# Weight sums for two units at once, sums as single steps, a narrower U-product, and a new order, in a kernel of local attention and a two-layer mixer

## The chip, the cores and the metric

The kernel runs on one core of one Trainium2 chip. The time is device microseconds of one execution. The kernel before took 217.62 us (median of 3 runs, 217.62 to 218.74). Its profiled execution took 217.54 us, of which 215.8 us lie between the first and the last recorded instruction (the span). The granted clock of TensorE was 1.000 in it.

## The reference

Attention over 4 batches of 8 heads, 768 positions and head size 64; each query sees the first 8 positions and the 96 up to its own, with a bias per head. Then a mixer over the 768 positions: a low-rank product with U (768 x 32) and V (32 x 768), and a two-layer MLP with 2048 hidden units.

```python
scores = scale * q @ k.T + bias                  # per head; bias = -slope * distance
scores = where(is_global | is_local, scores, -1e9)
a = softmax(scores)
x = (a @ v)                                      # heads side by side: (4, 768, 512)
h = x.transpose(0, 2, 1) @ U @ V
u = x + h.transpose(0, 2, 1)
out = u + relu(u @ w_ch1) @ w_ch2                # w_ch1: 512 x 2048, w_ch2: 2048 x 512
```

Inputs and output are float32; the kernel computes in fp16 with float32 accumulation.

## The kernel before

**How the order comes about.** The program makes a list of named tasks, each on one engine. `ORDER` is a written list of all names, and the instructions are issued exactly in this order: each engine takes its own in that sequence, and waits where data or a buffer is missing. `SLOTS` gives each task that takes a buffer or a PSUM bank the number of it. `CFG` names by one letter the engine (A for ACT, D for DVE, S for SyncE's DMA queue) of each movable task. A change of order is therefore a change of these three lists. The durations in the calls of `add` steer nothing on the chip.

**Attention**, for 16 pairs p of heads (four per batch). `lk`, `lq` and `lv` load k, q and v (POOL issues; pair 0's k and q come over SyncE). `Ck0` and `Cq0` cast pair 0. `TK` and `TQ` transpose on TensorE into PSUM and `EK`, `EQ` copy out (pairs 8 to 15 are transposed by DMA instead); `KO`, `VC` and `VG` build shifted copies with the global keys. `SB` adds the bias (batch 0), `S` makes scores in PSUM (line 652), `EX` is the exponential (ACT, line 717), `MK` the mask on DVE, `PV` the product with v (lines 780 and 781), `RC` and `NM` the normalization (DVE, lines 815 and 819), `XC` the cast to fp16.

**The low-rank mixer**, per pair. `UP` multiplies with U: six matmuls (line 764) with the 128-column U tile `uz` as the stationary and the 128 columns of x as the moving operand, which leave U^T x with 128 rows in PSUM; in batches 0 and 1 six more (line 759) transpose x. `TE` copies the result into `tmp` (ACT or DVE), `HM` multiplies with V (line 871), and `E0`, `E1` add or copy the sum into `uT`. In batches 2 and 3 `XT` transposes x by DMA.

**MLP-1** makes 16 blocks of 128 hidden units for 768 positions, in halves of 384. Plain blocks are `M1a` to `M1d` with relu `RL`, `RM` (batch 0 but for one unit). The others go in units z, each for the blocks z and z + 8, by a scheme of seven products instead of eight (`ZP1` to `ZP7`, two matmuls of 384 columns each, line 1024). It needs sums of the inputs (`ZT`, four DVE instructions in one task per batch, lines 979 to 982) and sums of the weights (`ZS`, four DVE instructions per unit, lines 1000 to 1003; made once per unit and kept). `ZU`, `ZW`, `ZX` and `ZR` copy PSUM out on ACT; `ZA`, `ZB` and `ZD` add with relu on DVE (line 1042) and free the bank.

**MLP-2** uses the same scheme once more: `PA` and `PB` (two DVE instructions each, four groups per batch) make sums of the relus, `TWa`, `TWb` sums of the second weights, `RS` starts the banks, `P1` to `P7` are products of eight matmuls each (line 1141), `DA` to `DH` add into the output on DVE (lines 1153, 1193), and `O` stores. `w` tasks are filler matmuls on zeros (line 1240).

```python
def sums_s(...):                     # ZS, one unit
    op(sw(2), a11, a21, ALU.subtract)
    op(sw(0), a21, a22, ALU.add)
    op(sw(1), sw(0), a11, ALU.subtract)
    op(sw(3), a12, sw(1), ALU.subtract)
```

Of the kernel before, what the change touches and what calls it, by code (L numbers as in the profile page):

```python
# [21 lines left out]
lk0 ones2 ones3 vz wz iota w6 lq0 ones0 relf w1 lk1 w4 rel3 bias1 bias0 w2 lq1 w0 w3 lk3 mask3 SB0.2 Ck0.0 Ck0.1 vs1  # L22
mask1 TK0 lv0 w7 Cq0.0 EK0.1 SB0.0 w5 mask7 lk2 Cq0.1 bias2 EK0.0 TQ0 lq3 SB0.1 KO0.1 EQ0.1 ones1 EQ0.0 KO0.0 lq2
S0.2 TK1 EX0.2 lv1 S0.1 EK1 TQ1 EX0.1 S0.0 lv2 EQ1 TK3 EX0.0 SB1.0 KO1 u16 SB1.1 bias4 S1.1 VC0 EK3 S1.0 vs0 uz SB1.2
VG0 lv3 EX1.0 KO3 S1.2 TK2 EX1.2 PV0 EK2 EX1.1 lk5 TQ3 RC0 NM0 TQ2 EQ3 SB2.1 KO2 SB2.2 EQ2 SB2.0 VC1 lk4 S2.0 VG1
S2.1 XC0 EX2.0 S2.2 PV1 EX2.2 VC2 lq4 SB3.1 uc EX2.1 RC1 back S3.1 mixl NM1 SB3.2 EX3.1 S3.2 VG2 lq5 SB3.0 VC3 VG3
S3.0 mask0 TK5 EX3.0 PV2 EK5 w1_1 EX3.2 PV3.0 RC2 UP0 RC3.0 w1_7 NM2 XC1 TK4 PV3.1 w1_5 TE0 EK4 PV3.2 XC2 HM0 RC3.1
lv4 RC3.2 UP1 NH3.1 E00 NH3.0 UP2 NM3 w1_3 TE1 UP3.0 TE2 UP3.1 NH3.2 w1_2 KO4 HM1 HM2 E01 TQ5 E02 w1_4 UP3.2 TQ4 TE3
EQ5 lk6 M1a0.3 EQ4 M1c0.3 HM3 S4.1 E13 E03 M1d0.3 EX4.2 lv5 ZT0 M1a0.2 M1c0.2 M1b0.3 EX4.1 w1_0 M1a0.15 RL0.3 M1b0.14
VC4 KO5 M1a0.14 RM0.14 w1_6 vs2 RL0.15 M1d0.2 mask2 S5.0 S4.0 M1b0.2 EX4.0 M1a0.11 EX5.0 MK4.0 M1b0.7 lk7 VG4 RL0.2  # L30
M1a0.7 MK4.2 RM0.7 MK4.1 M1b0.15 RL0.14 ZS3 M1b0.10 RL0.11 mask5 M1b0.6 MK5.0 RL0.7 RM0.15 lq7 ZS7 S5.1 RM0.10
M1b0.11 EX5.2 ZS6 PV4 w2_3 EX5.1 M1a0.10 lq6 RM0.11 M1b0.8 MK5.1 RM0.6 M1a0.8 RC4 RL0.10 NM4 VC5 ZP10.5 w2_1 ZP20.5
RM0.8 ZS5 M1a0.6 ZU0.5 RL0.8 M1a0.1 MK5.2 w2_2 mask6 TK6 M1c0.1 RL0.6 EK6 w2_0 ZP60.5 M1d0.1 TD0 ZW0.5 PA0.3 M1b0.1
lv6 VG5 M1b0.12 PA0.1 ZP50.5 RM0.12 M1b0.4 RL0.1 TK7 ZA0.5 RM0.4 ZP70.5 lq8 PB0.1 PV5 mask4 KO6 M1a0.5 EK7 ZX0.5 RC5
M1a0.4 lk9 NM5 RL0.5 TQ6 RL0.4 TQ7 ZB0.5 KO7 M1a0.12 EQ6 XC5 M1a0.0 EQ7 M1c0.0 lv8 PB0.3 ZP40.5 XC4 ZP30.5 M1d0.0
RL0.12 ZD0.5 M1b0.0 ZR0.5 M1b0.5 RL0.0 PA0.2 S7.0 lv7 RM0.5 UP4 EX7.0 PA0.0 S6.1 TE4 RS0.1 EX6.2 HM4 PB0.2 P20.1 E04
PB0.0 UP5 EX6.1 P10.1 TWa1 lk8 TE5 S6.0 RS0.0 EX6.0 HM5 DA0.1 P20.0 TWa0 lv9 VC6 P30.0 E05 lq10 TWb0 P50.0 VG6 P50.1
TWb1 lq9 P30.1 DF0.0 P60.1 MK6.1 TK8 P10.0 DF0.1 lk10 ZS2 S7.1 VG9 EX7.1 RS0.2 MK6.0 P10.2 DA0.0 EX7.2 MK6.2 P20.2
TQ8 DC0.1 VC7 PV6 MK7.2 VG7 TK9 P60.0 DB0.1 MK7.0 DA0.2 P70.1 RC6 TQ9 DB0.0 MK7.1 P60.2 DD0.1 NM6 PV7 TQ10 P40.1 RC7
XC6 NM7 VC9 lq12 P30.2 DB0.2 XC7 VG8 ZS4 UP6 KO8 UP7 lv11 DG0.1 DF0.2 TE6 P70.0 TE7 ZS1 lk11 HM7 HM6 S8.0 E07 E06  # L40
P50.2 DD0.0 lv14 DC0.0 E17 ZP11.6 KO9 ZT1 ZP11.7 lk12 P70.2 ZU1.7 ZU1.6 ZP21.7 EX8.0 P40.0 lq11 ZA1.7 ZP61.7 DG0.0
# [30 lines left out]
ZP53.4 ZR3.5 ZP53.7 ZX3.4 ZP23.3 ZB3.7 ZP13.0 ZR3.2 ZP63.3 ZB3.4 ZP63.1 ZA3.3 ZP23.2 ZP33.7 ZU3.0 ZA3.2 ZP53.2 ZW3.1
ZP43.4 ZD3.7 ZP33.4 TD3 ZW3.3 ZP23.1 ZD3.4 ZP63.0 ZP73.1 ZA3.1 ZW3.0 ZP53.1 ZB3.2 ZX3.1 ZP73.3 ZP73.0 PA3.3 ZX3.3
ZP23.0 ZR3.4 ZP33.2 ZP53.0 ZX3.0 ZB3.1 ZP53.3 ZD3.2 ZP43.3 ZP33.1 ZB3.0 ZR3.3 ZP43.0 ZB3.3 ZP43.1 ZR3.0 ZP33.0 ZD3.1
ZR3.1 ZP33.3 ZA3.0 RS3.0 RS3.2 ZD3.3 RS3.1 ZD3.0 P23.2 PA3.2 P13.0 PA3.0 P23.1 PA3.1 P23.0 P13.1 PB3.1 P53.2 DA3.1
DA3.0 P13.2 PB3.3 P63.0 DF3.2 PB3.0 P53.0 DA3.2 PB3.2 P63.1 O3.2a O2.2 P63.2 DB3.0 O2.5 O2.3 P53.1 DB3.2 O2.0 P33.1
DB3.1 P73.2 DF3.1 P33.2 DC3.2 DD3.2 P33.0 DC3.0 O3.5a P73.1 DF3.0 P73.0 O3.0 DD3.1 DC3.1 P43.2b DH3.2 O3.1 P43.1
DG3.2b DD3.0 O3.2 P43.2a O3.5c DG3.1 P43.0 O3.4 DG3.2a O3.5b w18 w8 DG3.0 w13 w11 O3.3 w17 w21 w14 w9 w15 w12 w16 w22
w19
""".split()  # L80
CFG = {
# [82 lines left out]
def kernel(  # L164
# [1127 lines left out]
```

## Time and profile before

| | |
|---|---|
| median of 3 runs | 217.62 us |
| profiled execution | 217.54 us |
| its span | 215.8 us |
| TensorE busy | 211.1 us (98%) |
| weight loads | 153.7 us (71%) |
| DVE busy | 189.3 us (88%) |
| ACT busy | 138.2 us (64%) |
| POOL busy | 72.2 us (33%) |

In the rows, a line begins with the line of the kernel, then the engine and the operation, what is written and read, the shape, the count, and then busy time and the mean of one in ns. In a timeline the first number is the start in us from the span's start and the second the duration. The chain of waits lists pieces as start, duration, and what ran. Matmuls are pipelined and their ends are modelled: a matmul's mean duration is longer than the distance from its start to the next one's.

### The profile page before, as it was taken

How to read it: one execution, taken by the hardware profiler on the slowest of the kernel's cores; microseconds unless marked ns; L12 is line 12 of the kernel's file. 1: busy time of each engine (PE TensorE's matmuls, PEld its weight loads, DVE VectorE, ACT ScalarE, POOL GpSimd, SP SyncE). 2: the span in 40 equal slices, each digit the busy share in tenths (PEclk: the TensorE clock that was granted, in tenths of full speed). 3: DMA queues.
4: the chain of work that ended last, by engine and by line, in shares of the span. 5: the costliest groups of instructions: out<-in, count | busy, mean ns of one | idle time of the engine just before them, and what ended most of it. 6: DMA issues, size and time to landing. Idle time of an engine off the chain costs nothing.

```text
span 215.8 us, 5747 instructions
## 1 busy us (share of the span) xinstructions
PE 211.1 (98%) x2298; PEld 153.7 (71%) x2298; DVE 189.3 (88%) x417; ACT 138.2 (64%) x255; POOL 72.2 (33%) x95
## 2 busy tenths in 40 slices
PE   8998999999999989999999999999999999999996
PEld 3565855676889866566787875667789766668896
DVE  4687977999999998999999899999999975999680
ACT  6999989989924669789886467785722068730000
POOL 8989967873670860013961100000000000000000
DMA  6999999999999999779999957651002310000543
GB/s 166 175 168 156 145 180 177 181 194 196 154 151 157 147 156 159 179 185 127 141 132 129 121 155 144 185 94 36 3 0 51 74 49 3 2 2 3 219 149 122
DMA packets 100731, 26.78 MB, mean 124 GB/s; under 512 B 87744, under 2 KB 98112, under 8 KB 100704
## 3 DMA queue, kind: packets, MB, share of 16 engines
q0 software_dynamic: 71312, 13.34, 80.1%
q1 hardware_dynamic: 29392, 13.07, 28.3%
q8 instruction: 18, 0.29, 0.6%
q14 instruction: 9, 0.07, 0.1%
HBM read 27.56 MB, written 6.29 MB: 157 GB/s over the span
## 4 chain that ended last, share of the span: by engine, by line
PE 91%; ACT 5%; DVE 2%; issue 1%; POOL 0%; POOLq 0%
PE ps L1141 35%; PE ps L1024 26%; PE ps L927 6%; PE ps L652 4%; ACT ep L717 4%; PE ps L1240 3%; PE ps L951 3%; PE ps L764 3%; PE ps L781 2%; PE ps L780 2%; PE ps L521 2%; PE ps L871 2%; PE ps L759 1%; PE ps L1133 1%; PE ps L633 1%
## 5 line engine op out<-in xcount | busy, mean ns | idle before, releaser
L717 ACT ACTIVATE ep<-ps 128x1024 f16<-128x1024 f32 (+1 forms) x48 | 43.9, 957 | 13.3 <-PE ps L652 12.5
L1141 PEld LDWEIGHTS <-htr 128*128 128x128 f16 x392 | 36.3, 98 | 7.3 <-issue 2.3
L265 ACT ACTIVATE zu<-ps 128x384 f32<-128x384 f32 x59 | 27.5, 491 | 8.5 <-PE ps L1024 7.6
L1042 DVE CUSTOM_DVE_ANT_0 htr<-ps,zu 128x384 f16<-128x384 f32 x59 | 31.0, 551 | 1.0 <-PE ps L1024 0.4
L1153 DVE TENSOR_TENSOR x_sb<-x_sb,ps 128x256 f32<-128x256 f32 (+1 forms) x60 | 27.1, 463 | 3.6 <-PE ps L1141 3.1
L1141 PEld LDWEIGHTS <-sA 128*128 128x128 f16 x288 | 27.5, 98 | 3.6
L364 POOL DMA_DIRECT2D vt<-in_v_dram x16 | 16.5, 1032 | 31.7 <-PE ps L781 22.4
L1024 PEld LDWEIGHTS <-w 128*128 128x128 f16 x200 | 18.9, 98 | 11.3 <-issue 0.2
L1141 PE MATMUL ps<-tB,htr 128*128 128x256 f16 (+1 forms) x200 | 24.0, 268 | 0.0
L1141 PE MATMUL ps<-w,sA 128*128 128x256 f16 x192 | 23.6, 273 | 0.0
L1141 PE MATMUL ps<-w,htr 128*128 128x256 f16 x192 | 23.5, 273 | 0.0
L360 POOL DMA_DIRECT2D stgq<-in_q_dram x24 | 19.9, 854 | 10.1 <-DMA qT<-stgq 7.2
L1024 PE MATMUL ps<-uT,w 128*128 128x384 f16 x100 | 23.0, 326 | 0.0
L1024 PE MATMUL ps<-zt,w 128*128 128x384 f16 x100 | 22.6, 326 | 0.0
L360 POOL DMA_DIRECT2D stgk<-in_k_dram x24 | 20.4, 872 | 4.1 <-DMA w<-in_moe_w_ch_dram 2.5
L265 ACT ACTIVATE x<-x_sb 128x768 f16<-128x768 f32 x13 | 10.9, 845 | 10.4 <-DVE x_sb L819 10.3
L730 DVE TENSOR_TENSOR ep<-ep,mask 128x1024 f16<-128x1024 f16 x24 | 16.3, 684 | 0.5 <-ACT ep L717 0.5
L819 DVE TENSOR_TENSOR x_sb<-ps,rcp 128x768 f32<-128x768 f32 x16 | 15.2, 952 | 0.3
L1024 PE MATMUL ps<-zt,zs 128*128 128x384 f16 x64 | 15.3, 326 | 0.0
L927 PE MATMUL ps<-uT,w 128*128 128x384 f16 x80 | 14.7, 326 | 0.0
L652 PE MATMUL ps<-qT,kT 64*128 64x128 f16 x192 | 14.1, 217 | 0.0
L652 PE MATMUL ps<-qT,kO 64*128 64x128 f16 x160 | 12.8, 218 | 1.0 <-DVE htr L1042 0.7
(119 smaller groups left out, 408.6 us busy)
## 6 DMA issues: line engine op xcount, KB each, us to landing
out_dram<-x_sb SPq DMA_DIRECT2D x20, 256.0 KB, 2.4
vt<-in_v_dram POOLq DMA_DIRECT2D x16, 192.0 KB, 7.0
stgk<-in_k_dram POOLq DMA_DIRECT2D x24, 96.0 KB, 6.0
stgq<-in_q_dram POOLq DMA_DIRECT2D x24, 96.0 KB, 5.6
w<-in_moe_w_ch_dram POOLq DMA_DIRECT2D x8, 256.0 KB, 8.6
w<-in_moe_w_ch_dram POOLq DMA_DIRECT2D x4, 512.0 KB, 9.8
out_dram<-x_sb SPq DMA_DIRECT2D x7, 128.0 KB, 2.2
vo<-vt SPq DMA_DIRECT2D x5, 123.8 KB, 2.5
```

Of the source, the lines that this page charges most:

```text
L265: nc.scalar.activation(dst, src, AF.Copy)
L360: nc.gpsimd.dma_start(o[:, i], src[b, h0 + i].rearrange("(n p) d -> p n d", p=P))
L364: nc.gpsimd.dma_start(vt[gv.slot][:, :, :, 0:D], v[b, h0:h0 + 2].rearrange("h (n p) d -> p h n d", p=P),)
L652: nc.tensor.matmul(t[:, hi, j * P:(j + 1) * P], lhs, qt[r, i * P:(i + 1) * P], start=not biased, stop=True, skip_group_check=biased,)
L717: nc.scalar.activation(ep[gep.slot][:, :, lo:512], ps[:, gsc.slot:gsc.slot + 2, lo:512], AF.Exp, scale=qk_scale)
L730: nc.vector.tensor_tensor(ev, ev, mv, ALU.mult)
L819: nc.vector.tensor_tensor(xo, pvo()[:, :, :, 0:D], rcp[p % 2].unsqueeze(3).broadcast_to((P, 2, NB, D)), ALU.mult)
L927: nc.tensor.matmul(ps[:, g.slot, 0:HS], w1[:, dc, jt * P:(jt + 1) * P], ub[:, dc, i * HS:(i + 1) * HS], start=(dc == 0), stop=(dc == NDC - 1),
L1024: nc.tensor.matmul(bank(g), a()[:, i], bq[:, i], start=first and i == 0, stop=last and i == 1, skip_group_check=True,)
L1042: return lambda: nc.vector._custom_dve(TENSOR_ADD_SAT, out=o, in0=x(), in1=y(), s0=3.0e38, s1=0.0)
L1141: nc.tensor.matmul(o if part is None else o[:, part], a[:, j, c0 + cols.start:c0 + cols.stop], bq[:, j] if part is None else bq[:, j, part ...
L1153: nc.vector.tensor_tensor(o, o, x, ALU.add)
```

## The change

- **Weight sums for two units.** The four steps of `ZS` become four tasks `ZYa` to `ZYd`, each for two neighbouring units (512 columns rather than 256), so 16 instructions instead of 32. They are kept in four tiles; `zt` takes over the early scratch space that lay in `once`.
- **Single steps.** `ZT` becomes `ZTa` to `ZTd`, `PA` and `PB` become `PA` to `PD`, `TWa` and `TWb` become `TWa` to `TWd`: the same instructions, each a task of its own in the order, and each product waits for the step it needs rather than for all.
- **The U-product with 32 moving columns**, for pairs 4 to 15 (`XU` in `CFG`): x is the stationary operand and 32 columns of U the moving one. `XE` (ACT, for pair 6 DVE) copies the 128 x 32 result four times side by side into `tmp`, `XU` turns it by one matmul with the identity, and `TE` copies as before.
- **A new order**, new slots and engines. Masks 0 and 1 stand ahead of the first exponential (before: 3, 1 and 7), the others in batch 0's MLP-1; `bias4` stands ahead of the first exponential.

```diff
+                    if xu:
+                        nc.tensor.matmul(
+                            ps[:, gx.slot, 384:384 + R], xx[:, c], uz[:, c, 0:R],
+                            start=xt and c == 0, stop=(c == NB - 1), skip_group_check=True,
+                        )
+                for c in () if xu else cs:
                     nc.tensor.matmul(
                         ps[:, gx.slot, 384:512], uz[:, c], xx[:, c],
...
+        if xu:
+            def xuevac():
+                copy(ENG[CFG["XE"][p]], tm.rearrange("p (g r) -> p g r", r=R), ps[:, gx.slot, 384:384 + R].unsqueeze(1).broadcast_to((P, P // R, R)))
+            def xuturn():
+                nc.tensor.matmul(ps[:, gx.slot + 1, 384:512], tm, ident16, start=xt, stop=True, skip_group_check=True)
+            XE = add(ENG[CFG["XE"][p]], 0.28, xuevac, [UP] + xw, name=f"XE{p}")
+            UP = add(PE, 0.06, xuturn, [XE], lat=0.3, name=f"XU{p}")
...
-            ZT = add(DVE, 2.21, sums_t, dd(range(NDC)) + zt_read, fast=32, name=f"ZT{b}")
+            for n, x, ch, dp in ((0, "a", (0, 1), ()), (2, "c", (0, 1, 2, 3), ()), (1, "b", (2, 3), (0,)), (3, "d", (2, 3), (1,))):
+                ZT[n] = add(DVE, 0.55, sums_t(n), dd(ch) + [ZT[i] for i in dp] + zt_read[n], fast=2, name=f"ZT{x}{b}")
...
+                for x, o, i0, i1, op in (
+                    ("a", zy[:, 1], c11, c21, ALU.subtract), ("b", c21, c21, c22, ALU.add),
+                    ("c", zy[:, 0], c21, c11, ALU.subtract), ("d", zy[:, 2], c12, zy[:, 0], ALU.subtract),
+                ):
...
+            for x, o, i0, i1, op, dp in (
+                ("A", s1, a21, a22, ALU.add, r21 + r22 + war(5)), ("C", s2, s1, a11, ALU.subtract, r11 + war(6)),
+                ("B", a21, a11, a21, ALU.subtract, r11 + r21), ("D", s4, a12, s2, ALU.subtract, r12 + war(3)),
+            ):
...
-    "TE": "AAADAAAAAAADAAAD", "EK": "ADDADDDDAADDAADD", "EQ": "DDAADADDADAAAAAA", "KO": "ADDDADAAAAAASSAD", "IB": "AAAA",
+    "TE": "DAADDAAAAADAAAAA", "EK": "ADDDADAAAADDAADD", "EQ": "DAAADDDAADAAAAAA", "KO": "AADDDDDAADAAAAAS", "IB": "AAAA",
-    "KOS": "DDDADADA", "VO": "DDDDDAAASSASASAS", "XC": "DAADAAAAAAAAAAAD", "E": "ADADAAADDDDDDDDD",
+    "KOS": "DDDADADA", "VO": "DDDDDAAAASASDDSA", "XC": "DDADDAAAAADAAAAA", "E": "AAADAAADDDDDDDDD",
```

The places of the order that the prediction's steps speak of, before and after (single lines of `ORDER`, cut):

```diff
-... TK0 lv0 w7 Cq0.0 EK0.1 SB0.0 w5 mask7 lk2 Cq0.1 bias2 EK0.0 TQ0 lq3 ...
+... w1 mask1 TK0 Cq0.0 Cq0.1 EK0.0 TQ0 EK0.1 lk2 KO0.0 SB0.0 ...
-... lv3 lk5 ... lk4 ... lq4 ... lq5 ... w1_1 w1_7 w1_5 lv4 ...          (POOL's loads)
+... lv3 lk4 lk5 w1_1 lq4 w1_7 lq5 w1_3 lv4 ...
-... HM7 HM6 S8.0 E07 E06 P50.2 DD0.0 lv14 DC0.0 E17 ZP11.6 KO9 ZT1 ZP11.7 ...
+... HM6 HM7 E06 ZYb0 ZP11.7 E07 P70.2 E17 DF0.2 ZU1.7 ZP21.7 O0.2 S8.0 ZA1.7 ZP11.6 EX8.0 VG9 lk15 ZTb1 ...
+... UP4 PD0.1 RM0.5 TWb0 lq8 S7.0 XE4 EX7.0 XU4 S6.1 TE4 PA0.2 HM4 ...
-... P43.2b DH3.2 O3.1 P43.1 DG3.2b DD3.0 O3.2 P43.2a O3.5c DG3.1 P43.0 O3.4 DG3.2a O3.5b w18 w8 DG3.0 w13 w11 O3.3 ...
+... O3.2 DG3.2a O2.4 P43.2b DD3.0 P43.1 O3.5b DG3.2b O3.5c P43.0 O2.1 DG3.1 O3.4 w19 w16 DG3.0 w9 w17 O3.3 ...
```

More of the change, by code (lines that the diff above doesn't have):

```diff
@@ L21 @@
 ORDER = """
[L22 to L41, printed above, removed]
@@ L72 @@
[L72 to L76, printed above, removed]
@@ L77 @@
-DB3.1 P73.2 DF3.1 P33.2 DC3.2 DD3.2 P33.0 DC3.0 O3.5a P73.1 DF3.0 P73.0 O3.0 DD3.1 DC3.1 P43.2b DH3.2 O3.1 P43.1
-DG3.2b DD3.0 O3.2 P43.2a O3.5c DG3.1 P43.0 O3.4 DG3.2a O3.5b w18 w8 DG3.0 w13 w11 O3.3 w17 w21 w14 w9 w15 w12 w16 w22
-w19
+lk0 wz iota w2 lq0 relf w4 lq1 w0 rel3 bias0 bias1 w7 lk1 bias2 w3 ones0 w5 lk3 mask0 SB0.2 Ck0.1 bias4 ones1 lv0
+Ck0.0 w1 mask1 TK0 Cq0.0 Cq0.1 EK0.0 TQ0 EK0.1 lk2 KO0.0 SB0.0 EQ0.1 KO0.1 SB0.1 lq3 EQ0.0 vz S0.2 lq2 EX0.2 TQ1 S0.0
+lv1 EQ1 TK1 SB1.2 EX0.0 EK1 vs1 S0.1 ones2 TK3 ones3 uz lv2 KO1 w6 EK3 SB1.0 EX0.1 S1.2 u16 S1.0 VC0 SB1.1 EX1.0 vs0
@@ new lines @@
+TK2 VG0 lv3 EX1.2 S1.1 EK2 PV0 EX1.1 TQ3 RC0 KO2 TQ2 NM0 lk4 SB2.2 EQ2 SB2.1 VC1 EQ3 SB2.0 VG1 S2.0 S2.1 lk5 EX2.0
+S2.2 KO3 PV1 XC0 EX2.1 RC1 SB3.1 uc EX2.2 w1_1 SB3.0 VC2 NM1 S3.0 S3.1 lq4 EX3.0 SB3.2 VG2 S3.2 EX3.1 VC3 UP0 XC1
+w1_7 EX3.2 PV2 TE0 VG3 lq5 TK4 RC2 PV3.0 NM2 EK4 PV3.1 PV3.2 TK5 RC3.0 RC3.1 XC2 HM0 RC3.2 w1_3 EK5 UP1 NH3.2 back
+E00 mixl lv4 UP2 NH3.0 NH3.1 TE1 UP3.0 NM3 TE2 w1_5 HM1 HM2 E01 UP3.1 KO4 lk7 UP3.2 TQ4 E02 TE3 M1a0.3 EQ4 M1c0.3
+ZTa0 HM3 S4.1 E13 E03 M1d0.3 EX4.2 KO5 M1a0.2 ZTc0 M1b0.3 lk6 M1c0.2 mask5 TQ5 RL0.3 M1a0.15 EQ5 mask6 M1a0.14 w1_6
@@ new lines @@
+EX4.1 M1b0.14 VC4 w1_2 RL0.15 M1d0.2 RM0.14 M1b0.2 w1_4 RL0.14 S4.0 ZYa3 S5.0 M1b0.6 ZYa1 EX5.0 M1a0.7 EX4.0 M1b0.15
+mask2 lq6 MK4.0 RL0.7 M1b0.11 vs2 RM0.15 M1b0.7 RL0.2 VG4 lv5 M1b0.10 MK4.1 RM0.6 mask3 S5.1 RM0.11 w1_0 MK5.0
+M1a0.10 RM0.7 ZYb3 RM0.10 lq7 PA0.1 TK6 EX5.1 M1a0.11 PC0.1 TK7 EX5.2 MK5.1 M1a0.4 w2_0 MK4.2 EK7 M1a0.5 w2_2 ZYa2
+PV4 RL0.11 MK5.2 w2_1 RL0.4 M1a0.6 PA0.3 RL0.10 w2_3 RC4 EK6 M1b0.12 PB0.3 NM4 VC5 lv10 M1a0.8 TQ6 TD0 VG5 ZTb0
+M1a0.12 RL0.6 PB0.1 PV5 RL0.5 XC4 mask4 EQ6 ZP10.5 RL0.12 M1b0.8 lk8 KO6 RM0.12 ZYb2 RL0.8 M1a0.1 ZYc3 M1c0.1 ZU0.5
@@ L872, in hmix @@
                     ps[:, gx.slot + half, 0:HS], tmp[b % 2][r, hp * P:(hp + 1) * P], vs[r, half],
-                    start=xt and half == 1, stop=True, skip_group_check=True,
+                    start=xt and not xu and half == 1, stop=True, skip_group_check=True,
                 )
@@ L1019, in bank, with pr @@
                 return ps[:, g.slot, 0:HS]
-            def pr(n, g, a, bq, dp, reads=False, first=False, last=False, z=z, gs=gs):
+            def pr(n, g, a, bq, dp, reads=False, first=False, last=False, z=z):
                 def go():
```

273 lines of the change are left out of this document (138 added, 135 removed), and 12 rows, old and new, of the table CFG.

## The prediction

> **What bounds the kernel now.** I read the page's first and fourth part, then the windows by stage, then the chain of waits, and where the chain leaves TensorE the timelines.
>
> ```profile
> span 215.8 us, 5747 instructions
> PE 211.1 (98%) x2298; PEld 153.7 (71%) x2298; DVE 189.3 (88%) x417; ACT 138.2 (64%) x255; POOL 72.2 (33%) x95
> ...
> PE 91%; ACT 5%; DVE 2%; issue 1%; POOL 0%; POOLq 0%
> ```
>
> TensorE carries the kernel; but DVE at 88% is close behind, and the chain leaves TensorE for ACT (5%, about 11 us) and for DVE (2%, about 4 us). The windows (busy us of PE, PEld, DVE, ACT, POOL) say where:
>
> ```profile
> 8.00:20.00 12.00, 11.72 (x217) 7.19 (x214) 10.28 (x25) 11.41 (x15) 10.57 (x14) 1.00 2.12 170
> 20.00:27.00 7.00, 6.56 (x123) 5.81 (x124) 5.76 (x15) 6.53 (x13) 7.00 (x10) 1.00 1.62 143
> 27.00:54.00 27.00, 27.00 (x280) 17.41 (x278) 23.80 (x58) 25.50 (x51) 17.73 (x22) 1.00 1.69 186
> 54.00:76.00 22.00, 21.96 (x272) 18.61 (x269) 21.48 (x49) 12.78 (x21) 12.90 (x16) 1.00 1.98 152
> 76.00:102.00 26.00, 25.18 (x230) 15.83 (x228) 24.52 (x54) 21.21 (x46) 5.83 (x7) 1.00 1.24 162
> 102.00:128.00 26.00, 25.96 (x334) 20.91 (x331) 24.75 (x48) 17.80 (x28) 11.31 (x14) 1.00 1.79 129
> ...
> 192.00:211.00 19.00, 19.00 (x187) 17.00 (x184) 15.94 (x36) 0.00 (x0) 0.00 (x0) 1.00 0.31 113
> ```
>
> From 8 to 20 us ACT is the fuller engine (11.41 of 12), and TensorE's 11.72 is many short matmuls whose modelled ends overlap. From 27 us on TensorE has no gap, except between 76 and 102 us (25.18 of 26). From 54 to 128 us DVE is 94 to 98% busy. So three things can shorten this kernel: fewer TensorE instructions after 20 us, less ACT work before 20 us, and less delay on DVE in the middle.
>
> **The change, part by part.** The sum is made against the profiled execution, 217.54 us, of which 215.8 are span; the median of the runs is 217.62, so the two stand for each other.
>
> *a. TensorE's work.* The rows are pieces of the chain (start, us, what, number of matmuls):
>
> ```profile
> 21.57 0.09 PE ps L781 x3
> ...
> 22.15 0.34 PE ps L764 x6
> ...
> 63.61 0.55 PE ps L652 x16
> ...
> 73.52 0.87 PE ps L1141 x8
> ...
> 210.76 3.06 PE ps L1240 x52
> ```
>
> The U-product of a pair is six matmuls of 128 moving columns, 0.34 us (L764), 0.057 each. With 32 columns the trace shows none; the nearest is PV with 65 columns, 0.03 each (L781), each with a weight load of its own. A matmul of 32 columns costs between 0.014 (a quarter of 0.057) and 0.057 (were the load the floor); I take 0.03, since the 65-column row shows that loads do not hold it above that. Twelve pairs: 12 x (0.34 - 0.18) = 1.9 us less. The turn back (XU) adds one matmul of 128 columns to each: 12 x 0.057 = 0.7. One filler task more (w15) stands in mid-order instead of behind the last product: four matmuls at 3.06/52 = 0.06, so 0.2. Sum -1.0; bounds +0.9 and -2.0. The Trainium skill, "TensorE: Matmul & The Clock Gate", on why the gap is 56 ns, puts a floor of about 25 ns under start-to-start however few the columns. By it the six would take an estimated 0.15 and this term be -1.4; no row here goes below 65 columns. The same page of the Trainium skill, on the back-to-back gap, gives about 81 ns per matmul for a stream of weight loads and matmuls of 128 columns. Row L764, with a load for each, shows 57, and the trace decides.
>
> *b. The first 20 us, ACT.* Pieces of the chain:
>
> ```profile
> 6.34 0.41 PE ps L1240
> ...
> 10.75 0.52 ACT once L316
> 11.26 0.70 ACT kT L265
> ...
> 15.91 0.48 issue
> ...
> 19.95 0.41 ACT mask L1228
> ```
>
> The new order puts TQ0 straight behind its casts, not behind a 512-column filler (-0.41). bias4 (-0.52) goes ahead of the first exponential, where ACT waits anyway; mask0 takes mask3's early place and leaves 19.95 (-0.41); EK3 goes to DVE (-0.70). EQ2 stands before EQ3, so that S2.0 no longer waits for the later of them (-0.48). Against that EQ1 and KO1 come to ACT:
>
> ```profile
> L265 ACT ACTIVATE qT<-ps 128x768 f16<-128x768 f16 x3 | 2.4, 847 | 0.0
> L265 ACT ACTIVATE kO<-kT 128x480 f16<-128x480 f16 x8 | 4.8, 602 | 0.0
> L265 ACT ACTIVATE kO<-kT 128x160 f16<-128x160 f16 x8 | 2.7, 333 | 0.0
> ```
>
> As back-to-back work I take 0.70 for EQ1 (the chain's piece for EK3, same shape) and 0.85 for KO1, a little under 0.60 + 0.33: +1.55. The sum is -0.97. Loads must follow: w1_1, which the first MLP-1 tile needs, moves ahead of lq4 and lq5 in POOL's queue, so it comes earlier, and they later; TQ4 and TQ5 stand later too. I take -0.9; bounds 0 (a load or the casts hold the stage) and -2.5 (EQ1 and KO1 fit into waits).
>
> *c. DVE, single steps and wider sums.* The timelines, DVE first, then TensorE (start, us):
>
> ```profile
> 78.30 0.55 DVE L981 TENSOR_TENSOR zt<-uT 128x768 f16<-128x768 f16 x1
> 78.77 0.55 DVE L982 TENSOR_TENSOR zt<-uT,zt 128x768 f16<-128x768 f16 x1
> 79.23 0.55 DVE L1042 CUSTOM_DVE_ANT_0 htr<-ps,zu 128x384 f16<-128x384 f32 x1
> ...
> 81.15 0.29 DVE L1001 TENSOR_TENSOR w<-w 128x256 f16<-128x256 f16 x1
> 81.47 0.29 DVE L1002 TENSOR_TENSOR once<-w 128x256 f16<-128x256 f16 x1
> 81.80 0.29 DVE L1003 TENSOR_TENSOR once<-w,once 128x256 f16<-128x256 f16 x1
> 82.01 0.55 DVE L1042 CUSTOM_DVE_ANT_0 htr<-ps,zu 128x384 f16<-128x384 f32 x1
> ```
> ```profile
> 78.95 0.23 PE L652 MATMUL ps<-qT,kO 64*128 64x128 f16 x1
> 79.83 0.21 PE L652 MATMUL ps<-qT,kO 64*128 64x128 f16 x1 [0.65 <-DVE htr L1042]
> ...
> 83.53 0.23 PE L652 MATMUL ps<-qT,kO 64*128 64x128 f16 x2 [0.17 <-DVE x_sb L1153]
> ```
>
> A step that needs the one just before it starts 0.32 to 0.33 after it (81.15, 81.47, 81.80); an unrelated one follows after 0.21 (82.01). So each dependent neighbour costs 0.11. A ZS of one unit holds DVE for 3 x 0.32 + 0.21 = 1.2 us, eight of them 9.4. Two units at once make 16 steps of 512 columns, an estimated 0.34 each (between 0.21 for 256 and 0.47 for 768, 78.30 to 78.77): 5.4, thus 4.0 less. In the new order only three steps stand right behind one that they need, of PA to PD, ZT and TW; the old PA and ZT had twenty such places, 2.2 us. The changed engine choices (four pieces of EK, EQ and E off DVE, some nine short ones of VO, XC, KO, TE and XE onto it) I count as nil. About 6 us of 189 go, all off the chain but in one place: at 78.95 S8.0 waits 0.65 for a bank that ZA1.7 (L1042) frees, which stood behind the ZT1 steps; at 83.53 S8.1 waits 0.17. In the new order S8.0 stands ahead of ZA1.7, and ZP5 waits for one step of ZT alone. I take -0.8 for these two and -0.5 for the hidden remainder of 54 to 128 us, where DVE had 1 to 6% of slack; bounds 0 and -2.5.
>
> *d. The second trip.* UP now goes through XE, XU and TE to HM. Before XU can start, UP's last matmul must end and XE run:
>
> ```profile
> L764 PE MATMUL ps<-x,uz 128*128 128x128 f16 x96 | 8.2, 219 | 0.0
> L265 ACT ACTIVATE tmp<-ps 128x128 f16<-128x128 f32 x13 | 3.7, 282 | 4.3 <-PE ps L764 4.2
> L717 ACT ACTIVATE ep<-ps 128x1024 f16<-128x1024 f32 x32 | 31.6, 1027 | 11.2 <-PE ps L652 10.9
> ```
>
> That is 0.22 + 0.28 = 0.50 us. TensorE's cover between UP and XU is one MLP-2 product (0.87) for pairs 5, 7, 9, 10, 11, 13 and 15, several ZP for 8 and 12, some 0.6 for 14; for pair 4 only S7.0, six matmuls at 0.034 (0.2): 0.3 uncovered. XE6 stands on DVE behind TWd0 and two more; 0.1 for it. Sum +0.4; bounds 0 and the rival below. XE also adds 11 x 0.28 = 3.1 us to ACT, idle for a third of the span.
>
> *e. The end.* Behind the last RS, DVE has 13 single steps of PA to PD among the DA and DB that free the banks; P63.2 waits for DA3.2, which stands behind five others after the last PC. DVE had 15.94 of 19.00 there, so the cover is thin: +0.3, bounds 0 and +1.0. The stores O2.0, O2.4 and O2.1 (256 KB each) move in among the last of SP's queue:
>
> ```profile
> out_dram<-x_sb SPq DMA_DIRECT2D x20, 256.0 KB, 2.4
> ```
>
> O3.4 and O3.3 wait behind O2.1. Its issue falls in the time of P43.0 (0.87), so I take nothing; if data queues, at most its 2.4.
>
> Sum: -1.0 - 0.9 - 1.3 + 0.4 + 0.3 = -2.5, **215.0 us** (span 213.3).
>
> **Rivals.**
>
> *Everything comes through.* The middle loses all 2.5 of c, ACT's stage 1.5, and the trip costs nothing: -1.0 - 1.5 - 2.5 + 0.3 = -4.7, 212.8. For it: 54 to 128 us has two full engines now. Against: few gaps are left to close. Chance 0.12.
>
> *ACT takes over in batch 0's MLP-1, and the gain stays there.* From 27 to 54 us ACT has 25.50 of 27.00. Between EX4.2 and RM0.5 the new order adds two masks, EK6, EK7 and EQ7, and takes out KO6, XC4 and XC5:
>
> ```profile
> L1228 ACT ACTIVATE mask<-once 128x384 f16<-128x384 f16 x8 | 4.3, 537 | 0.8 <-DVE once L304 0.8
> L265 ACT ACTIVATE kT<-ps 128x768 f16<-128x768 f16 x1 | 0.8, 823 | 0.0
> L265 ACT ACTIVATE x<-x_sb 128x768 f16<-128x768 f32 x13 | 10.9, 845 | 10.4 <-DVE x_sb L819 10.3
> ```
>
> That is 2 x 0.54 + 2 x 0.82 + 0.85 - 0.94 - 2 x 0.85 = +0.9, so 26.4 of 27. It decides where a relu comes late by more than its bank's turn. Then b's 0.9 is waited out there, and up to 1.0 on top: 217.54 - 2.5 + 1.9 = 216.9. The same place holds the case that the change doesn't do what it says: 32 columns cost 0.057 each, term a is +0.9, and the time 216.9. The PV row speaks against that. Chance of both, 0.16.
>
> *Slower: XE waits behind exponentials.* ACT takes its instructions in order; an exponential (1.03) just ahead of XE makes the trip 1.53, of which 0.87 is covered: 0.66 per pair. Without d the sum is -2.9; the loss must pass 4.0, so it decides at six of twelve pairs. At eight it is 5.3: 217.54 - 2.9 + 5.3 = 219.9. For it: ACT waited 4.2 us for just such products (L265 tmp), so the chain is short of slack. The Trainium skill, "Perfetto Trace Analysis", on the Tensor Engine instruction in its lifecycle part, says that ACT's and DVE's queues never reorder; the wait at 78.95, behind DVE's steps, agrees. The order speaks against it: an exponential stands directly ahead of XE only at pairs 5 and 11. Chance 0.14.
>
> **How the numbers follow.** A measurement here can tell about 0.5%, 1.1 us, from no change. Forecast 0.58 (213.4 to 216.5), everything 0.12, ACT or no saving 0.16, slower 0.14. So faster 0.58 + 0.12 = 0.70, the same 0.16, slower 0.14. The range leaves out the slower case and half of the first rival: 212.8 to 217.9.
>
> **What would show it.** Right: L764's successor takes 0.18 us for six; MLP-1's first piece starts about 0.9 us earlier; no wait of S8 on L1042; DVE's busy time 1 to 3 us lower, with fewer starts 0.32 apart; XU shows gaps of 0.3 at pair 4 only. Wrong: TensorE waiting for XE at several pairs, ACT full with TensorE gaps from 27 to 54 us, TensorE gaps after 190 us, or 32-column matmuls at 0.05.

## The result, and the profile after

The changed kernel takes 215.65 us (median of 18 runs, 215.01 to 217.62), the kernel before 217.82 (18 runs beside it, 217.39 to 221.14): ratio 0.9899, 95% interval 0.9879 to 0.9918. It is about 2.2 us faster; 215.0 was forecast.

The first profiled execution of the changed kernel was the slowest of its 18 (217.62 us), so the lines here are those of another execution of the same kernel, which took 215.56 us, unless the text says otherwise. Line numbers are those of the changed kernel: scores 654, UP's transposition 762 and its 32-column matmul 767, XU 877, HM 890, ZT 1001, ZY 1029, ZP 1044, ZA to ZD 1062, PA to PD 1115, MLP-2's products 1149, DA to DH 1161, stores 1216, fillers 1248, E08 and the like 898, copies on ACT 267 and on DVE 269.

The page, first and fourth part:

```profile
span 213.7 us, 5781 instructions
...
PE 209.3 (98%) x2310; PEld 152.0 (71%) x2310; DVE 185.3 (87%) x407; ACT 141.7 (66%) x267; POOL 72.7 (34%) x95
...
PE 86%; DMA 7%; DVE 2%; POOL 1%; ACT 1%; issue 1%; DVEq 0%
```

TensorE and DVE are both less busy (211.1 and 189.3 before). ACT has left the chain (5% before, 1% now) and DMA has come into it. The windows (busy us of PE, PEld, DVE, ACT, POOL):

```profile
8.00:20.00 12.00, 11.82 (x216) 7.31 (x212) 9.62 (x22) 11.79 (x16) 11.20 (x16) 1.00 2.03 159
20.00:27.00 7.00, 7.00 (x133) 5.76 (x130) 6.59 (x21) 5.79 (x10) 7.00 (x9) 1.00 1.62 152
27.00:54.00 27.00, 26.90 (x277) 17.57 (x272) 21.83 (x51) 26.50 (x52) 18.84 (x23) 1.00 1.67 186
...
76.00:102.00 26.00, 26.00 (x250) 16.95 (x250) 24.26 (x51) 23.24 (x48) 8.20 (x10) 1.00 1.46 178
102.00:128.00 26.00, 25.56 (x331) 20.72 (x332) 25.20 (x53) 16.83 (x29) 7.35 (x9) 1.00 1.36 130
```

From 76 to 102 us TensorE is without a gap in this execution (25.18 of 26 before); from 102 to 128 it has lost a little (25.96 before). From 27 to 54 ACT stands at 26.50 of 27, and TensorE at 26.90.

The same by stages of the kernel. A stage ends where TensorE starts its first MLP-1 matmul, the first matmul of RS in each batch, and the last product. Its work is the count of matmuls of each form by the usual distance from one start to the next of that form; what is left are waits. Differences in us, after less before:

| stage | before | after | work | waits |
|---|---|---|---|---|
| to the first MLP-1 matmul | 26.85 | 25.64 | -0.34 | -0.87 |
| to RS of batch 0 | 26.82 | 27.43 | +0.38 | +0.23 |
| to RS of batch 1 | 48.07 | 46.30 | -0.65 | -1.12 |
| to RS of batch 2 | 46.83 | 47.21 | -0.20 | +0.58 |
| to RS of batch 3 | 42.82 | 42.13 | -0.85 | +0.16 |
| to the last product | 19.10 | 19.35 | +0.32 | -0.07 |
| from there to the end | 5.28 | 5.65 | | +0.37 |
| span | 215.77 | 213.71 | -1.34 | -0.72 |

Work and waits are good to about 0.1 us a stage. The +0.32 before the last product is two MLP-1 matmuls that the new order issues behind RS of batch 3 instead of ahead of it. The two other profiles of the changed kernel have the same work, but other waits: to RS of batch 1 they take 46.60 and 47.65 us, to RS of batch 2 46.89 and 46.91. So of the 1.12 us that the waits to RS of batch 1 lose here, some 0.8 are lost in one of them and none in the other.

The TensorE timeline shows the new U-product and its turn, and then the place where S8 waited 0.65 us before:

```profile
51.45 0.22 PE L762 MATMUL ps<-ident,x 128*128 128x128 f16 x1
51.51 0.18 PE L767 MATMUL ps<-uz,x 128*128 128x32 f16 x1
51.53 0.22 PE L762 MATMUL ps<-ident,x 128*128 128x128 f16 x1
51.59 0.18 PE L767 MATMUL ps<-uz,x 128*128 128x32 f16 x1
...
51.90 0.22 PE L654 MATMUL ps<-qT,kT 64*128 64x128 f16 x2
52.22 0.23 PE L877 MATMUL ps<-ident,tmp 128*128 128x128 f16 x1
...
77.98 0.23 PE L654 MATMUL ps<-qT,kO 64*128 64x128 f16 x2
...
81.14 0.23 PE L654 MATMUL ps<-qT,kO 64*128 64x128 f16 x2
```

A 32-column matmul takes 0.02 to 0.03 us of TensorE (51.51 to 51.53); six without transpositions between them, as from pair 8 on, take 0.153 from the first start to that of the next matmul. Behind the scores at 51.90 TensorE stands 0.28 us longer than usual until XU4 (52.22). Both scores of pair 8 (77.98, 81.14) start without a wait here. On DVE the sums of ZT now stand one by one among other work:

```profile
76.76 0.55 DVE L1001 TENSOR_TENSOR zt<-uT,zt 128x768 f16<-128x768 f16 x1
77.23 0.41 DVE L1161 TENSOR_TENSOR x_sb<-x_sb,ps 128x256 f32<-128x256 f32 x1
77.56 0.55 DVE L1001 TENSOR_TENSOR zt<-uT 128x768 f16<-128x768 f16 x1
78.03 0.41 DVE L1161 TENSOR_TENSOR x_sb<-x_sb,ps 128x256 f32<-128x256 f32 x1
```

This isn't so in each execution. In the first profiled one, TensorE has gaps from 76 to 102 us, and DVE waits there for the transposition of pair 9's keys by DMA:

```profile
76.00:102.00 26.00, 24.95 (x238) 15.89 (x237) 23.03 (x51) 22.93 (x48) 5.93 (x7) 1.00 1.66 169
```
```profile
DVE kO L269 <- DMA kT<-stgk: 1.9, 1, 1.9
```

The change moved this copy, KO9, from ACT to DVE. While it waits at the head of DVE's queue, the last sum of ZT and an addition that frees a bank stand behind it. A product then waits 0.38 us for that sum, and the second scores of pair 8 wait 0.62 for the bank (0.17 before). Eight profiles have this part of the new order: the three of the changed kernel and those of five runs below (without the narrow U-product, with two waits mended, with the first 20 us as before, and the two with the stores moved). In four of them KO9 waits, for 0.5 to 2.2 us; in the four profiles of the old order DVE has no such wait.

The new wait, from 102 us on, is read from the chain (start, us, what):

```profile
94.92 0.74 PE ps L1044 x5
95.67 5.42 DMA uT<-x
...
101.21 0.95 DVE uT L898
102.16 0.94 DVE sA L1115 x2
103.10 0.47 DVE htr L1115
103.57 0.99 DVE sA L1115 x3
104.57 0.33 issue
104.89 0.42 DVE x_sb L1161
105.32 0.04 issue
105.36 1.91 PE ps L1149 x16
```

Pair 8's transposition by DMA took 5.42 us (4.98 in the kernel before). E08 (line 898) needs it, and behind E08 DVE does six sums before DA, which frees the bank for the product at 105.36. TensorE loses 0.38 in front of 102.2, where the next scores wait for E08, and 0.40 in front of 105.36. In the two other profiles, where the six sums stand in the same place, the waits of this stage are 0.3 us up on the kernel before.

### The profile page after: what moved, and what is told of

Read it like the earlier page. It is cut to its first block, busy times and chain, and to the rows that moved or that the text cites. A ratio compares the mean times of both kernels' runs of the same rounds, so it can differ in the third digit from the quotient of the medians.

```text
span 215.8 us, 5781 instructions
## 1 busy us (share of the span) xinstructions
PE 209.7 (97%) x2310; PEld 151.9 (70%) x2310; DVE 184.7 (86%) x407; ACT 142.2 (66%) x267; POOL 72.7 (34%) x95
## 4 chain that ended last, share of the span: by engine, by line
PE 87%; DMA 6%; DVE 3%; issue 1%; POOL 1%; ACT 1%; DVEq 0%; POOLq 0%
PE ps L1149 33%; PE ps L1044 25%; PE ps L949 6%; DMA vt<-in_v_dram 4%; PE ps L654 4%; PE ps L1248 3%; PE ps L973 2%; PE ps L789 2%; DMA uT<-x 2%; PE ps L788 2%; PE ps L523 2%; PE ps L890 2%; PE ps L762 1%; PE ps L1141 1%; PE ps L635 1%; DVE sA L1115 1%
## 5 line engine op out<-in xcount | busy, mean ns | idle before, releaser
L1149 PEld LDWEIGHTS <-sA 128*128 128x128 f16 x288 | 27.1, 98 | 4.1 <-issue 0.4
L1161 DVE TENSOR_TENSOR x_sb<-x_sb,ps 128x256 f32<-128x256 f32 (+1 forms) x60 | 26.8, 460 | 3.3 <-PE ps L1149 3.1
L1149 PE MATMUL ps<-w,sA 128*128 128x256 f16 x192 | 24.1, 273 | 0.2 <-DVE x_sb L1161 0.2
L1149 PE MATMUL ps<-w,htr 128*128 128x256 f16 x192 | 24.0, 273 | 0.0
L1044 PE MATMUL ps<-zt,zs 128*128 128x384 f16 x76 | 17.6, 326 | 0.0
L267 ACT ACTIVATE x<-x_sb 128x768 f16<-128x768 f32 x11 | 9.3, 846 | 10.1 <-DVE x_sb L827 10.1
L1044 PEld LDWEIGHTS <-zs 128*128 128x128 f16 x114 | 10.9, 98 | 7.1
L789 PEld LDWEIGHTS <-ep 128*128 128x128 f16 x192 | 12.4, 97 | 2.2 <-issue 0.6
```

The lines of the kernel that those rows point to most:

```text
L267: nc.scalar.activation(dst, src, AF.Copy)
L789: nc.tensor.matmul(o, e[:, hi, (j + 1) * P:(j + 2) * P], vv[:, hi, i, 0:D1], start=(i == 0), stop=True)
L1044: nc.tensor.matmul(bank(g), a()[:, i], bq[:, i], start=first and i == 0, stop=last and i == 1, skip_group_check=True,)
L1149: nc.tensor.matmul(o if part is None else o[:, part], a[:, j, c0 + cols.start:c0 + cols.stop], bq[:, j] if part is None else bq[:, j, part ...
L1161: nc.vector.tensor_tensor(o, o, x, ALU.add)
```

## The experiments

**Once more.** The changed kernel itself, beside the other runs, on two chips:

> The changed kernel once more, for a profile of an ordinary execution (the first one's time, 217.62 us, is the highest of its runs). Time 215.3 to 216.0 us. My theory (the sum of the prediction): against the kernel before, batch 1's RS starts 0.5 to 1.5 us earlier, batch 2's and 3's RS 1.5 to 2.5 us earlier, and the time from the last product to the end is unchanged, within 0.3 us. Rival (the tail): the RS marks differ by under 1 us and the end behind the last product is shorter by over 1 us.

> The changed kernel itself, beside the other runs on the same chip: 215.4 to 215.9. The tail from the last product to the end is 5.7 us; the stores' effect is read from the difference to this.

Measured: 215.87 us, ratio 0.9908 (0.9877 to 0.9939), and 215.61, ratio 0.9911 (0.989 to 0.9931). Three profiles of this one kernel start MLP-1 at 26.70, 25.52 and 25.64 us, so what happens before that scatters by 1.2 us between executions. The stage to RS of batch 1 scatters as much (46.30 to 47.65), the others less, and the one to RS of batch 3 is 42.13 in all three. In the profile of the first of these two runs RS of batches 1, 2 and 3 starts 1.6, 1.6 and 2.3 us earlier than before, about as the theory said; but the end behind the last product is 0.43 us longer, where 0.3 at most was expected.

**Without the narrow U-product.**

```diff
-    "XU": (4, 5, 6, 7, 8, 9, 10, 11, 12, 13, 14, 15),
+    "XU": (),                                  # and no XE, XU in ORDER
```

> The changed kernel with the U-product as before (128 moving columns, no XE and XU), all else of the new order kept. Theory: TensorE has 12 x (0.34 - 0.18 - 0.06) = 1.2 us more to do and no second trip; 0.8 to 1.2 us slower than the changed kernel, 216.4 to 216.9. Rival 1 (the trip eats what the narrower product saves): 215.4 to 215.9, the same. Rival 2 (the U-product is the whole gain): 217.6, as the kernel before.

Measured: 217.45 us, ratio 0.9972 (0.9955 to 0.9989), 1.6 more than the changed kernel on the same chip (215.87). Of its page:

```profile
PE 210.8 (98%) x2298; PEld 153.2 (71%) x2298; DVE 186.3 (86%) x406; ACT 139.1 (64%) x256; POOL 72.7 (34%) x95
```

TensorE is back at 210.8. In the new order the U-product carries 1.6 of the 1.9 us by which the changed kernel gained there (217.76 to 215.87). That is above the theory's 0.8 to 1.2 and close to the second rival. It is what TensorE's work gives with the measured 0.15 us: 12 x (0.34 - 0.15 - 0.06) = 1.6. Everything else, the wide sums, the single steps, the new order and the end together, is worth 0.3 us in this run (0.2 to 1.0 by the interval); b, c, e and the filler of the prediction add up to 1.7.

**The wide sums alone, in the old order.**

```diff
-... ZS3 M1b0.10 RL0.11 ... ZS7 S5.1 ...       # one unit, 256 columns a step
+... ZYa3 ZYb3 ZYc3 ZYd3 ...                   # two units, 512 columns a step, together
```

Two plain blocks of batch 0, 8 and 12, change places with it, so that both units of a sum are ready.

> The order, slots and engines of the kernel before, with the weight sums of two units at once (four steps standing together, at the place of one of the pair's two), and every other sum's steps also standing together as before; the U-product as before. In batch 0 the plain blocks 8 and 12 change places, so that the pair 4, 5 can be summed in time. Theory: DVE gets some 4 us of work less, little of it on the chain: 0 to 0.8 us faster than the kernel before, 217.0 to 217.8. Rival (the wide sums carry the gain): 216.0 or less.

Measured: 218.13 us, ratio 1.0009 (0.9988 to 1.003). DVE's busy time fell from 189.3 to 187.7, not by the 4 us that were expected, and the time stayed. In its profile neither of the two waits in front of S8 is there, and the stage to RS of batch 1 is 0.56 us shorter than before; but the one to RS of batch 0 is 1.03 longer, most of it a wait of TensorE for a load of MLP-1's weights:

```profile
PE ps L948 <- DMA w<-in_moe_w_ch_dram: 0.9, 1, 0.9
```

Whether the exchange of the two blocks makes this wait is not shown.

**The same with single steps.** Every step that stood right behind the one it needs was moved up to three places down DVE's queue:

```diff
-EX4.2 lv5 ZTa0 ZTb0 ZTc0 ZTd0 M1a0.2 ...
+EX4.2 lv5 ZTa0 M1a0.2 ... VC4 ZTb0 ZTc0 ZTd0 KO5 ...
```

> The last one, with each dependent step moved at most three places down on DVE, so that another instruction stands between it and the step it needs (38 such neighbours become 1). Nothing else differs. Theory: each neighbour cost 0.11 us on DVE, 4.1 us in all; where DVE holds TensorE (76 to 84 us) and from 54 to 128 us that brings 0.4 to 1.0 us over the last one. Rival (DVE is off the chain all but there, and later steps cost what separation saves): within 0.2 us of the last one.

Measured: 222.19 us, ratio 1.0193 (1.0165 to 1.022): 4.1 us slower than with the steps together, though DVE was busy 2.8 us less (184.9). Neither theory nor rival foresaw that. Its DVE timeline, and the TensorE instruction that came late:

```profile
31.68 0.33 DVE L268 COPY vo<-vt 128x660 f16<-128x660 f16 x1 [2.78 <-DMA vt<-in_v_dram]
31.93 0.55 DVE L1000 TENSOR_TENSOR zt<-uT,zt 128x768 f16<-128x768 f16 x1
...
33.33 0.41 DVE L268 COPY kO<-kT 128x480 f16<-128x480 f16 x2
...
33.80 0.23 PE L653 MATMUL ps<-qT,kO 64*128 64x128 f16 x2 [1.67 <-DVE kO L268]
```

VC4 waits 2.78 us for its load (0.61 in the run with the steps together); three sums that used to be done in that time now stand behind it, and the kO copy behind them, so TensorE waits 1.67. The Trainium skill, "Perfetto Trace Analysis", on the Tensor Engine instruction in its lifecycle part, says that these queues never reorder; this row agrees. Another 1.2 us goes where a product waits for a weight sum that was moved down:

```profile
PE ps L1043 <- DVE zs L1028: 1.2, 1, 1.2
```

**The new order with the steps put together**, at the earliest place that the buffers allow, and then at the latest:

```diff
-S7.1 ZTa1 EX7.1 ...                            # ZTb1, ZTc1, ZTd1 further down
+EX8.0 VG9 lk15 ZTa1 ZTb1 ZTc1 ZTd1 P40.0 ...  # earliest
+ZU1.6 VC8 ZTa1 ZTb1 ZTc1 ZTd1 ZP61.7 ...      # latest
```

> The changed kernel with its single DVE steps put back together: the four sums of ZT, ZY, TW and the two of PA+PC and PB+PD stand side by side again at the place of one of them, so that 37 steps instead of 5 follow directly on the step that they depend on. Everything else, the wide sums and the 32-column products included, stays. If the free places of the steps are worth what term c of the prediction says, this takes 0.5 to 1.3 us more than the changed kernel (216.2 to 217.2 where that one takes 215.7), and DVE is busy about 2 to 3 us longer; the new gaps of TensorE stand in front of products that wait for a DVE sum. Rival: the steps by themselves are worth nothing, since TensorE is filled and DVE has slack; then 215.5 to 215.9, with DVE busy longer all the same.

> As the run with the steps put together at the earliest place (226.5, 10.7 us slower), but with each group at the latest place of one of its steps at which the order stays possible, so that no group stands in DVE's queue before its data are there. If what cost 10.7 us was the blocked queue (sums waiting at its head) and the steps themselves are worth 0.5 to 1.3, this takes 216.3 to 217.5. Rival: products that wait for late sums cost as much as a blocked queue does, so that it is the whole placement and not the steps; then 219 or more, with the gaps of TensorE in front of the products.

Measured: 226.54 us, ratio 1.0402 (1.0373 to 1.043), and 234.04, ratio 1.0747 (1.0728 to 1.0766). DVE is busy 189.1 in both, 3.8 more than in the changed kernel for 32 more steps that directly follow one they need: 0.12 each. TensorE's waits of over 0.15 us add up to 8.4 and 15.7 us (1.5 in the changed kernel). The two largest that the placement makes (us in total, times, longest), first of the earliest, then of the latest place:

```profile
PE ps L1149 <- DVE x_sb L1161: 1.7, 2, 0.9
PE ps L1044 <- DVE htr L1062: 1.2, 4, 0.4
```
```profile
PE ps L1149 <- DVE sA L1115: 5.4, 7, 1.1
PE ps L1044 <- DVE zt L1001: 2.3, 2, 1.3
```

Put early, the sums hold up the additions that free TensorE's banks (lines 1161 and 1062); put late, the products wait for the sums themselves (1115 and 1001). Of the first run neither theory nor rival holds. Of the second the rival does: the placement costs 11 to 18 us, far more than the 3.8 us that the steps take longer. So these runs price two placements; what single steps are worth by themselves they don't show.

**The U-product alone, in the old order with the wide sums.**

```diff
-UP9 DF1.0 VG10 PV11 MK10.2 TE9 ...
+UP9 XE9 DF1.0 VG10 PV11 MK10.2 XU9 TE9 ...    # and so for pairs 4 to 15
```

> The order of before with the wide sums (the kernel that took 218.13, no different from before) and with nothing more than the 32-column U-product: each pair of batches 1 to 3 gets its small copy right behind UP and its turn behind at least 0.55 us of other TensorE work, the head mix behind at least 0.45. If the U-product's saving is independent of the order, this takes 1.0 to 1.8 less: 216.3 to 217.1, TensorE's busy time 1.0 to 1.5 lower. Rival: in an order that wasn't planned for it the second trip through ACT and DVE costs as much as it saves (the copies stand behind exponentials); then 217.8 to 219.

Measured: 220.31 us, ratio 1.0123 (1.0107 to 1.0138), 2.2 more than without it (218.13). The rival holds here. By the stages, worked out as above, TensorE's work fell by 1.5 us, and its waits grew by 3.5. The longest of them that are new or longer here:

```profile
PE ps L1044 <- ACT uT L267: 0.9, 1, 0.9
PE ps L1149 <- DVE x_sb L1161: 0.6, 1, 0.6
PE ps L1141 <- ACT ep L719: 0.5, 1, 0.5
```

These are matmuls behind copies, additions and exponentials; that these come later because of the second trip's copies in the same queues is argued, not shown.

**Two waits of batch 0 mended.** In the first of the two further profiles the query load of pair 5 was late, in the timeline of TensorE:

```profile
28.91 0.49 PE L523 MATMUL ps<-ident,stgq 128*128 128x128 f16 x6 [0.45 <-DMA stgq<-in_q_dram]
```

```diff
-mask5 TQ5 RL0.3 M1a0.15 EQ5 mask6 M1a0.14 ...
+mask5 RL0.3 M1a0.15 TQ5 mask6 M1a0.14 EQ5 ...
-XE4 EX7.0 XU4 S6.1 TE4 PA0.2 HM4 EX6.1 RS0.1 PA0.0 P10.1
+XE4 EX7.0 S6.1 XU4 TE4 PA0.2 EX6.1 RS0.1 PA0.0 P10.1 HM4
```

> The changed kernel with the two places of batch 0 mended at which its gain was lost: the transposition of the fifth pair's queries, which waits 0.6 us for its load at 28.1, is issued after the second plain MLP-1 block, and the small turn of pair 4 (52.35, 0.28 us behind its ACT copy), its copy and its head mix each stand one product group later. If these two waits are on the path, the start of batch 0's weight sums (53.5 us) comes 0.6 to 0.9 earlier and the total is 0.5 to 0.9 below the changed kernel's (about 215.0). Rival: what is given early is only moved, since DVE or ACT is what batch 0 runs at; then the gap reappears further down in the same batch and the total stays within 0.2.

Measured: 215.81 us, ratio 0.9911 (0.9878 to 0.9943): no gain. In its profile neither wait is there, but in front of RS a new one of 0.46 stands, and the wait at 28 us is absent also from the second further profile of the unchanged order. It belonged to one execution. The gap in front of XU4 is in all three profiles of the changed kernel; taking it away only brought the one in front of RS.

**The first 20 us as before.** ACT's share of the new order taken back:

```diff
-... mask0 SB0.2 Ck0.1 bias4 ... EQ0.0 vz S0.2 ... KO1 w6 EK3 SB1.0 EX0.1 S1.2 ...
+... mask0 SB0.2 Ck0.1 ... EQ0.0 mask5 vz S0.2 ... KO1 w6 SB1.0 EX0.1 bias4 EK3 S1.2 ...
                                    # EK3 on ACT; EQ1 and KO1 on DVE
```

> The changed kernel with ACT's first 20 us put back nearly as before: a third mask (0.52) in front of the first exponential, the 0.62 us bias copy and a kT copy (0.82) in front of pair 1's first exponential, and one qT and one kO copy moved from ACT to DVE in exchange. Term b says that the first exponential decides the start of MLP-1: the first M1 block then starts 0.5 to 0.9 us later than in the changed kernel (25.5 to 26.2 or 26.4 in the profile) and the total is 0.5 to 0.9 higher, about 216.4. Rival: this time is swallowed in batch 0 (by the wait for the query load at 28.1, which stays where it is); then the first M1 block is later and the start of the weight sums at 53.5 is not, and the total is the same within 0.3.

Measured: 216.10 us, ratio 0.993 (0.9903 to 0.9958). In its timeline of ACT the mask stands in front of the first exponential again, and the 512-column copy and the kT copy before the later ones:

```profile
7.72 0.52 ACT L1235 ACTIVATE mask<-once 128x384 f16<-128x384 f16 x1
8.14 1.73 ACT L718 ACTIVATE ep<-ps 128x1024 f16<-128x1024 f32 x2
...
11.10 0.62 ACT L317 ACTIVATE once<-once 128x512 f16<-128x512 f16 x1
11.62 0.80 ACT L266 ACTIVATE kT<-ps 128x768 f16<-128x768 f16 x1
```

MLP-1 starts at 26.64, a time that the changed kernel itself had in one of three profiles. The median is 0.2 to 0.5 higher than the changed kernel's three, with intervals that overlap: for term b, but it doesn't settle it. More comes from the profiles together. Nine have the changed kernel's order up to MLP-1, which starts at 25.5 to 27.1 us in them, median 25.75; four have the old one, 26.8 to 27.2, median 26.9.

**Three stores out of the way.**

```diff
-... DF3.1 O2.0 P63.0 ... DG3.2a O2.4 P43.2b ... P43.0 O2.1 DG3.1 O3.4 ...
+... ZP53.7 DG2.1 O2.1 O2.4 O2.0 ZX3.7 ...     # before batch 3's products
```

> The changed kernel with the three last stores of batch 2 (rows 0, 1 and 4) issued as soon as their sums are there, before batch 3's products, and no more between the stores of batch 3; only the queue of SP changes. The prediction held these stores for free and put 0.3 on the end for other reasons. If the stores between those of batch 3 are what made the end 0.44 us longer (5.72 us from the last product to the end of the span, 5.28 before), the tail is 0.3 to 0.5 shorter and the total about 215.4. Rival: the last store's own way decides (the wait of 0.9 from issue to its neighbours in the queue), then the tail stays at 5.7 and nothing changes within 0.2.

Measured: 214.74 us, ratio 0.9871 (0.9837 to 0.9904), a gain of about twice what was expected. Timelines of the end, the last four products and then the last store, in the kernel before:

```profile
210.16 0.60 PE L1141 MATMUL ps<-tB,htr 128*128 128x256 f16 x4
...
211.24 1.26 SPq L1208 DMA_DIRECT2D out_dram<-x_sb  x1
```

in the changed kernel:

```profile
207.73 0.60 PE L1149 MATMUL ps<-tB,htr 128*128 128x256 f16 x4
...
208.82 1.19 SPq L1216 DMA_DIRECT2D out_dram<-x_sb  x1
```

and with the stores moved (its profiled execution began MLP-1 at 27.11 and took 216.54, so only its end is compared):

```profile
209.79 0.60 PE L1149 MATMUL ps<-tB,htr 128*128 128x256 f16 x4
...
210.88 0.82 SPq L1216 DMA_DIRECT2D out_dram<-x_sb  x1
```

The last store is issued 1.08 to 1.09 us after those products start, in all three. From its issue to the end of the span it is 4.5 us before (215.77 - 211.24), 4.9 in the changed kernel (213.71 - 208.82) and 3.9 here (214.77 - 210.88). The last 1.2 us of it, from the landing of the data to the end, are the same in all three; the landing comes 3.3, 3.7 and 2.7 us after the issue. The large stores from 206.3 us on show it (KB each, median us from issue to landing), first in the changed kernel, then with the stores moved:

```profile
out_dram<-x_sb SPq DMA_DIRECT2D x4, 256.0 KB, 3.8
```
```profile
out_dram<-x_sb SPq DMA_DIRECT2D x3, 256.0 KB, 2.7
```

How long the issue itself takes (1.26, 1.19, 0.82) is not what decides: in the profile of the run with the two waits mended, which has the stores of the changed kernel, it took 0.33 us, and the data landed 3.85 us after its start.

**The stores and the query transposition together.** The two edits of ORDER shown above, without that of XU4.

> The changed kernel with the three last stores of batch 2 issued before batch 3's products (as in the run of the stores, 214.74) and, besides, the transposition of the fifth pair's queries behind the second plain MLP-1 block, where it waits for no load (as in the run with the cover, where the weight sums of batch 0 began 0.6 us earlier in the profile and the median stayed). If both are on the path: 214.1 to 214.5. Rival: the wait of 0.6 at 28.1 is made good again later in most executions, then 214.6 to 214.9, as with the stores alone.

Measured: 214.59 us, ratio 0.9855 (0.9837 to 0.9873), where the changed kernel had 0.9911 on the same chip: 1.0 us faster than it, 3.2 faster than before. Beside the run with the stores alone (0.9871) nothing more is to be seen: the rival, as the run with the two waits mended says.

## Why the prediction was right, point by point

- **a, TensorE's work, -1.0.** Right in cause, and too small: the work is 1.34 less. The six narrow matmuls take 0.153 us, 0.18 was forecast. The prediction's estimate by the floor of the Trainium skill, "TensorE: Matmul & The Clock Gate", on why the gap is 56 ns, was 0.15, and -1.4 for the term; this trace shows 0.025 per matmul and agrees with that floor of about 25 ns. Leaving the U-product out gives back 1.6 us. The filler in mid-order is there, ahead of the first RS of batch 2.
- **b, the first 20 us, -0.9.** The stage's waits are 0.87 less in the profile compared here. The same kernel began MLP-1 1.1 us later in another execution, and the run that takes b back costs 0.2 to 0.5 with overlapping intervals; but the medians of nine profiles and of four are 1.2 us apart (0.34 of it is work that moved behind), which bears the size out. How much of it reaches the end is another matter: without the U-product the kernel gained 0.3 us in all.
- **c, DVE, -1.3.** The step that was mis-sized. In the profile compared here the two waits in front of S8 went as said (-1.12 between the first RS of batches 0 and 1, the forecast for the two being -0.8). But the -0.5 for a remainder that DVE hides did not come: in the next stage +0.58 came instead, where E08 waits for a DMA and DA stands behind six sums. That makes -0.54. The profile of the first repeat gives about the same (-0.81 and +0.26), but the first profile of the kernel +0.52 (+0.24 and +0.28). What came out differently there is a part that the prediction counted as nil, the changed engine choices: KO9, now on DVE, waits for its DMA and holds up what stands behind it. The cause isn't shown either: wide sums alone leave the time as it was, though the waits in front of S8 are gone in their profile too, and in the two orders tried single steps cost 4.1 us or save 11 to 18, by where they stand. DVE's busy time fell by 4.0 us (189.3 to 185.3), where about 6 was worked out. The 0.11 us per dependent neighbour is real DVE time (0.12 in the run with the steps together), but little of it is TensorE's time.
- **d, the second trip, +0.4.** 0.28 at pair 4, for which 0.3 was said; the 0.1 for XE6 isn't there. In an order not planned for it, the same trip costs more than it saves (+2.2).
- **e, the end, +0.3.** +0.37, near the number by luck, since the reason given isn't it. P63.2 doesn't wait: the stage to the last product lost 0.07 of waits. What the prediction took at nothing, the stores of batch 2 among the last ones, is all of it and more: taking them out saves 1.0 (some of batch 2's stores stood there before, too). O3.3 isn't issued later, as was considered (0.76 us after the last product starts, before and after); its data land later: 3.67 us from issue, 3.31 before, which is the whole of the +0.37, and 2.68 with the stores moved.
- **The rivals.** "Everything comes through" failed at c. ACT did fill batch 0's MLP-1 to 26.50 of 27.00, close to the 26.4 worked out, but TensorE is busy 26.90 there: its gap is XU4's. Exponentials in front of XE cost nothing to be seen in the new order.

The forecast is 0.65 lower than the measured time. That it is no further off is in part luck: a brought 0.3 us more than its term and c 0.8 less, in the profile compared here. The run without the U-product says the same more sharply: the U-product with its second trip was forecast at -0.8 and brought -1.6; all the rest, the filler included, was forecast at -1.7 and brought -0.3.

## What to carry to other kernels

Where each engine takes its instructions in order, a step is worth what stands behind it in its queue: price a re-ordering from those queues, not from the engine's busy time. Transfers that look free beside the last compute step are not, when their data are still in flight as the last store is issued: 1 us here. An instruction that can wait for a DMA holds up all that stands behind it on its engine, so moving it to the engine that TensorE waits for is a change with a price. And before a wait is mended, or a gain is put down to a change, look whether a second execution of the same kernel has it.

## What was not expected of the hardware

The last store's own way depends on what is in flight: with 256 KB stores between the last ones its data landed 3.6 to 3.9 us after its issue in six profiles, with these stores moved 2.6 to 2.7 in two. An execution's first 25 us scatter by more than 1 us with the loads (in the first profile of the changed kernel TensorE waits 0.39 and 0.29 us for loads of q and k at 8 to 9 us, in the one compared here for none), and a transposition by DMA near 80 us is on time in one execution and holds DVE up for 1.9 us in another, while a stage at 150 us repeats to 0.01 us.
